# Attention with two expert layers on one core: a list schedule that prices the shared SBUF port and a half clock at the start

## The chip, the cores and the metric

The kernel runs on one core of a Trainium2 chip. The metric is the device time of one execution in microseconds (us), the median of several runs. Engines are named as in the profile: PE is TensorE's matrix multiply and PEld its weight load, DVE is VectorE, ACT is ScalarE, POOL is GpSimd, SP is SyncE, which issues the DMAs.

## The reference

B = 4 batches, 8 heads, 576 positions, 64 columns per head; q and k are drawn eight times larger than v.

```python
# pooled attention: mean over 4 neighbours, softmax attention on 144 positions, repeated 4 times
q_d = q.reshape(B, H, Sd, factor, D).mean(axis=3)      # the same for k_d, v_d
out_up = np.repeat(sm_attn(q_d, k_d, v_d), factor, axis=2)
# local attention: a band of 7 keys around each position
mask = np.abs(pos[:, None] - pos[None, :]) < factor
out_local = softmax(np.where(mask, q @ k.T / 8, -1e9)) @ v
x = (out_up + out_local)                               # as 2304 tokens x 512
...
h = x @ w_in;  g = s * relu(h) ** 2 + b;  y = g @ w_out        # layer 1, 512 -> 2048 -> 512
h = y @ w_in2; g = h - np.tanh(h);        out = g @ w_out2     # layer 2, the same sizes
```

## The kernel before

The 2304 tokens are worked in eight blocks u of 288. Each block's x is written as two parts, xh (high) and xl (low, what xh leaves over), so that products of a faster number format keep their accuracy; X[u] is ready when the last xl is written. Blocks 0 and 1 are one batch, whose attention runs on TensorE with narrow products at the start: transposes tokT of the loaded q and k (L543), scores S (L573, L575) and pooled scores Sd (L614), transposed softmax weights PT and PdT (L588, L634), products with V O and up (L598, L644), and the transposes xt (L655). Among these stand warm-ups (warm, L853), products of the identity with itself whose result isn't used: 14 at first and 16 later, where the kernel's text places them. Each is two rows of the trace.

For blocks 2 to 7 the local attention runs elementwise. VectorE makes most products of Q and K (pD, L181), GpSimd some (pP, L181), VectorE sums both by rows into s (L186), then come a softmax and the products with V (pD and pP at L249, pA on ScalarE at L245), which VectorE adds into O (L257). The pooled attention of these batches takes reductions pp (L353), maxima nm (L398) and sums E on VectorE. At the end xq adds both (L314) and VectorE subtracts xl (L318).

Layer 1 runs on TensorE while later blocks are still in attention: ph is x times the first weights (L735, twelve products per slice i of 128 hidden columns: xh, xl with the two parts of the weight), ScalarE squares the relu into gh, VectorE makes its low part gl (L756), and acc collects gh and gl times the second weights (L768), which yst takes away (L783 to L791). The weights are split into their parts at L697 to L723. Layer 2 (L1000 to L1016 and L735 for yxh, yxl) follows behind 600 us.

Every engine executes its own list in order. These lists are not the order of the text: list_schedule reckons through the whole program with one cost per instruction from cost(), takes for each engine that comes free the ready instruction of the highest priority (the text's place), and pin_order makes the resulting order binding. What it reckons decides only the order; when an instruction really starts, semaphores decide. The words of the start and the warm-ups' places stand in these lines:

```python
RING = '0p1s2ps'
WARM0 = 14
WARM_AT = 'efpu'
...
def warm(n):
    for _ in range(n):
        pe.matmul(warm_t[:, :128], ident, ident, start=True, stop=True)
```

and what a round of list_schedule picks, in these:

```python
_, n = heapq.heappop(ready[e])
i = by[n]
order[e].append(n)
```

Of the kernel before, what the change touches and what calls it, by code (L numbers as in the profile page):

```python
# [1066 lines left out]
ENG = {"PE": 55, "Activation": 34, "DVE": 33, "Pool": 78, "SP": 30}  # L1067
ISSUE = 450.0
BW = 300.0


def cost(i, reads, writes):
    e = i.engine.name
    w = writes[0]
    n = 1
    for ap in [*reads, *writes]:
        k = 1
        for _, c in list(ap.ap)[1:]:
            k *= c
        n = max(n, k)  # L1080
    if i.opcode == "DMACopy":
        return ISSUE, 0.0
    if e == "PE":
        n = 1
        for _, c in list(w.ap)[1:]:
            n *= c
        if "float32r" in str(reads[0].dtype):
            t = (n + 32) / 2.4
        elif i.is_transpose:
            t = 64.0 if n <= 72 else 110.0  # L1090
        else:
            t = 1.2 * n
        return t, t + 162
    if e == "Activation":
        t = 170 + 0.85 * n
        if len([r for r in reads if r is not reads[0]]) and n < 200:
            t += 115
        return t - 110, t
    if e == "DVE":
        t = 140 + 1.05 * n  # L1100
        if i.opcode == "TensorReduce" and list(reads[0].ap)[-1][0] != 1:
            t *= 1.7
        return t - 80, t
    t = 140 + 2.35 * n
    return t - 60, t


def issue_order(tc, nc):
# [129 lines left out]
def list_schedule(ins, dep, soft, aps):  # L1238
    import heapq
    by = {i.name: i for i in ins}  # L1240
    eng = {n: i.engine.name for n, i in by.items()}
    left = {n: len(d) + len(soft[n]) for n, d in dep.items()}
    nxt = {n: [] for n in dep}
    for n, d in dep.items():
        for m in d:
            nxt[m].append((n, False))
        for m in soft[n]:
            nxt[m].append((n, True))
    ready, later = {e: [] for e in ENG}, {e: [] for e in ENG}
    free, at, order = {e: 0.0 for e in ENG}, {n: 0.0 for n in dep}, {e: [] for e in ENG}  # L1250
    key = {i.name: (i.bass_priority, k) for k, i in enumerate(ins)}
    wake = [(0.0, e) for e in ENG]
    dma = 0.0
    for n in by:
        if not left[n]:
            heapq.heappush(later[eng[n]], (0.0, key[n], n))
    heapq.heapify(wake)
    while wake:
        t, e = heapq.heappop(wake)
        if t < free[e]:  # L1260
            continue
        while later[e] and later[e][0][0] <= t:
            _, k, n = heapq.heappop(later[e])
            heapq.heappush(ready[e], (k, n))
        if not ready[e]:
            if later[e]:
                heapq.heappush(wake, (later[e][0][0], e))
            continue
        _, n = heapq.heappop(ready[e])
        i = by[n]  # L1270
        order[e].append(n)
        if i.opcode == "RegisterMove":
            busy, end = 30.0, t
        else:
            busy, end = cost(i, *aps[n])
            end += t
        if i.opcode == "DMACopy":
            size = 4
            for _, c in list(aps[n][1][0].ap):
                size *= c  # L1280
            dma = max(dma, t + 1300.0) + size / BW
            end = dma + 900.0
        free[e] = max(t + busy, dma - 2000) if e == "SP" else t + busy
        heapq.heappush(wake, (free[e], e))
        todo = list(nxt[n])
        while todo:
            m, order_only = todo.pop()
            if m not in by:
                left[m] -= 1
                if not left[m]:  # L1290
                    todo += nxt[m]
                continue
            if order_only:
                go = t
            elif eng[m] == e and i.opcode != "DMACopy":
                go = t if e == "PE" else end + 32
            else:
                go = end + ENG[eng[m]]
            at[m] = max(at[m], go)
            left[m] -= 1  # L1300
            if not left[m]:
                heapq.heappush(later[eng[m]], (at[m], key[m], m))
                heapq.heappush(wake, (max(at[m], free[eng[m]]), eng[m]))
    assert sum(map(len, order.values())) == len(ins)
    return order


def pin_order(tc, nc):
    ins, dep, soft, aps = issue_order(tc, nc)
    order = list_schedule(ins, dep, soft, aps)  # L1310
    by = {i.name: i for i in ins}
    behind = mybir.DependencyInfo(mybir.DependencyClass.NoSync, mybir.DependencyReason.DATA)
    for l_ in order.values():
        for a, b in zip(l_, l_[1:]):
            tc.add_manual_dep(by[b], a, behind, reason="issue order")
# [30 lines left out]
```

## Time and profile before

| what | before |
|---|---|
| median of three runs | 976.96 us |
| the runs | 973.97, 976.96, 979.11 us |
| the profiled execution's own time | 974.62 us |
| its span (first to last instruction) | 972.8 us |
| TensorE busy | 929.2 us, 96% |
| VectorE busy | 616.8 us, 63% |
| ScalarE busy | 453.3 us, 47% |
| GpSimd busy | 166.4 us, 17% |

The span is what the trace shows; 1.8 us of the execution's own time lie around it. The share of an engine is a mean over the whole span and hides stages: VectorE is full in the first 40% and half idle later. An instruction's duration in the trace is from its start to its end, so it holds what it waits inside for something shared.

### The profile page before, as it was taken

Reading aid. Unit: us, or ns where it says so; the run is one execution under the profiler, and the core shown is the slowest. Engines: PE = TensorE matmul, PEld = TensorE weight load, DVE = VectorE, ACT = ScalarE, POOL = GpSimd, SP = SyncE. Lnnn points to the kernel's source line nnn. Section 1 sums busy time; section 2 is a strip of 40 time slices with the busy share of each in tenths; the row PEclk is TensorE's granted clock in tenths of the full one; section 3 lists DMA queues with packets and bytes.
Section 4 is the critical chain, followed back from the end, with each engine's and each line's share of the span. In section 5 each row is a group of like instructions: output and inputs, shape, how many; then the busy total and the mean of one; then the engine's idle time right before and its main releaser. Section 6 shows DMA issues by size and latency. Waiting matters only on the chain.

```text
span 972.8 us, 15109 instructions
## 1 busy us (share of the span) xinstructions
PE 929.2 (96%) x5786; PEld 830.7 (85%) x5786; DVE 616.8 (63%) x966; ACT 453.3 (47%) x1216; POOL 166.4 (17%) x128
## 2 busy tenths in 40 slices
PE   9989999899899899899999999999999999999998
PEld 8778988799788789899899989888888888888886
DVE  5788899999999999996775983322332232222222
ACT  5789746345547374556585962221322232122221
POOL 1553533233225233251000000000000000000000
PEclk9579999999999999999999999999999999999999
DMA  9990323223130322310173850000110000001001
GB/s 232 308 356 2 130 87 126 78 86 126 54 126 26 96 84 78 101 54 1 47 260 136 322 144 11 22 1 1 43 44 1 1 26 19 0 1 44 1 1 43
DMA packets 57966, 80.72 MB, mean 83 GB/s; under 512 B 21046, under 2 KB 42790, under 8 KB 57894
## 3 DMA queue, kind: packets, MB, share of 16 engines
q1 hardware_dynamic: 57510, 79.24, 25.5%
q8 instruction: 45, 0.74, 0.3%
q10 hardware_dynamic: 384, 0.52, 0.2%
q14 instruction: 27, 0.22, 0.1%
HBM read 69.72 MB, written 10.03 MB: 82 GB/s over the span
## 4 chain that ended last, share of the span: by engine, by line
PE 70%; DVE 20%; issue 5%; ACT 3%; POOL 0%; DMA 0%; SPq 0%; DVEq 0%; POOLq 0%; ACTq 0%
PE ph L735 33%; PE acc L1016 20%; PE acc L768 11%; DVE O L257 2%; DVE s L186 2%; DVE pD L181 2%; DVE pp L353 2%; DVE gl L756 2%; DVE xq L314 1%; DVE pD L249 1%; DVE wf L715 1%; DVE xl L318 1%; PE warm L853 1%; DVE O L249 1%; PE O L598 1%
## 5 line engine op out<-in xcount | busy, mean ns | idle before, releaser
L735 PE MATMUL ph<-xh,w 128*128 128x288 f32 x1024 | 239.3, 307 | 7.6 <-DVE gl L756 6.1
L768 PE MATMUL acc<-gh,w 128*128 128x288 f32 (+1 forms) x1024 | 228.1, 298 | 3.7 <-DVE yst L791 2.1
L735 PE MATMUL ph<-yxh,w 128*128 128x512 f32 (+1 forms) x640 | 194.0, 369 | 0.0
L1001 DVE TENSOR_TENSOR ph<-ph,th 128x512 f32<-128x512 f32 (+1 forms) x80 | 51.5, 645 | 224.0 <-ACT th L1000 224.0
L735 PEld LDWEIGHTS ph<-xh,w 128*128 128x128 f32 x1024 | 176.6, 194 | 16.0 <-DVE gl L756 9.2
L1016 PE MATMUL acc<-w,gx 128*128 128x512 f32 x768 | 185.4, 391 | 0.0
L768 PEld LDWEIGHTS acc<-gh,w 128*128 128x128 f32 x1024 | 171.7, 189 | 6.1 <-DVE yst L791 3.0
L1016 PEld LDWEIGHTS acc<-w,gx 128*128 128x128 f32 x768 | 144.2, 188 | 31.2
L735 PE MATMUL ph<-xl,w 128*128 128x288 f32 x512 | 156.2, 305 | 8.6 <-DVE xl L318 6.4
L1000 ACT ACTIVATE th<-ph 128x512 f32<-128x512 f32 (+1 forms) x80 | 44.4, 555 | 232.7 <-PE ph L735 232.6
L768 PE MATMUL acc<-gl,w 128*128 128x288 f32 x512 | 151.2, 296 | 0.0
L735 PEld LDWEIGHTS ph<-yxh,w 128*128 128x128 f32 x640 | 116.9, 188 | 21.8
L735 PE MATMUL ph<-yxl,w 128*128 128x512 f32 (+1 forms) x320 | 118.3, 370 | 0.0
L735 PEld LDWEIGHTS ph<-xl,w 128*128 128x128 f32 x512 | 99.1, 193 | 10.9 <-DVE xl L318 7.1
L768 PEld LDWEIGHTS acc<-gl,w 128*128 128x128 f32 x512 | 97.0, 190 | 0.0
L747 ACT ACTIVATE ph<-ph 128x288 f32<-128x288 f32 x128 | 51.0, 398 | 88.3 <-PE ph L735 88.2
L756 DVE TENSOR_TENSOR gl<-ph,gh 128x288 fp32r<-128x288 f32 x128 | 57.2, 449 | 31.9 <-ACT gh L753 31.3
L735 PEld LDWEIGHTS ph<-yxl,w 128*128 128x128 f32 x320 | 60.2, 188 | 10.7
L1003 DVE TENSOR_TENSOR gx<-ph,gx 128x512 fp32r<-128x512 f32 x64 | 44.2, 690 | 37.8 <-ACT gx L1002 37.8
L245 ACT ACTIVATE pA<-V,a 128x64 f32<-128x64 f32 x198 | 53.7, 343 | 11.3 <-DVE O L257 10.5
L1002 ACT CAST gx<-ph 128x512 fp32r<-128x512 f32 x64 | 37.5, 586 | 44.9 <-DVE ph L1001 44.9
L753 ACT CAST gh<-ph 128x288 fp32r<-128x288 f32 x128 | 50.9, 398 | 7.0 <-PE acc L768 4.1
(137 smaller groups left out, 1200.1 us busy)
## 6 DMA issues: line engine op xcount, KB each, us to landing
wraw<-in_moe_w_in_dram SPq DMA_DIRECT2D x32, 512.0 KB
wraw<-in_moe_w_out_dram SPq DMA_DIRECT2D x32, 512.0 KB
y<-yst SPq DMA_DIRECT2D x36, 144.0 KB
K<-in_k_dram SPq DMA_DIRECT2D x5, 960.0 KB
V<-in_v_dram SPq DMA_DIRECT2D x5, 960.0 KB
Q<-in_q_dram SPq DMA_DIRECT2D x6, 576.0 KB
raw<-in_q_dram SPq DMA_DIRECT2D x24, 144.0 KB
raw<-in_k_dram SPq DMA_DIRECT2D x24, 144.0 KB
```

Source lines behind the costliest of these rows:

```text
L181: eng.tensor_tensor(out=p, in0=Qt[u], in1=Kt[u][:, :, o:o + TAU, :], op=ALU.mult)
L245: act.activation(out=p_[:, t, h], in_=Vt[u][:, h, o + t], func=AF.Copy, scale=st["a"][:, h * TAU + t, o:o + 1])
L735: pe.matmul(p_, w_, x_, start=n == 0, stop=n == 3 * KC - 1)
L747: act.activation(out=p_, in_=p_, func=AF.Relu)
L753: act.copy(out=gh[:, :NB1], in_=p_)
L756: dve.tensor_tensor(out=gl, in0=p_, in1=gh[:, :NB1].bitcast(F32), op=ALU.subtract)
L768: pe.matmul(accs[u][e][:, :g_.shape[1]], w_, g_, start=i == first and n == 0, stop=i == last and n == 2)
L1000: act.activation(out=t, in_=p_, func=AF.Tanh)
L1001: dve.tensor_tensor(out=p_, in0=p_, in1=t, op=ALU.subtract)
L1002: act.copy(out=gh, in_=p_)
L1003: dve.tensor_tensor(out=gl, in0=p_, in1=gh.bitcast(F32), op=ALU.subtract)
L1016: pe.matmul(accs[j][t], g_, w_, start=i == 0 and n == 0, stop=i == NF - 1 and n == 2)
```

## The change

Only the planner changes; the program's instructions are the same. Three things: cost() gets other numbers for ScalarE, VectorE, GpSimd and Memset. The new takes_port() marks the instructions of VectorE and GpSimd that the planner shall let run in turn only: all of GpSimd's but Memset, and VectorE's that touch no PSUM and are no TensorReduce or Reciprocal. While one of them is reckoned to hold the port (held), the other engine takes the best ready instruction that needs no port, or waits; VectorE also gives way where GpSimd has a ready one of higher priority. And up to COLD = 55 us every cost of TensorE counts twice.

```diff
+COLD = 55000.0
...
+    if i.opcode == "Memset":
+        return 50 + 0.8 * n, 100 + 0.8 * n
+    last = [d for d in list(reads[0].ap)[1:] if d[1] > 1]
+    strided = bool(last) and abs(last[-1][0]) > 2
     if e == "Activation":
-        t = 170 + 0.85 * n
-        if len([r for r in reads if r is not reads[0]]) and n < 200:
+        t = 160 + 0.85 * n
+        if len(reads) == 2:
             t += 115
+        elif len(reads) > 2:
+            t += 190
         return t - 110, t
     if e == "DVE":
-        t = 140 + 1.05 * n
-        if i.opcode == "TensorReduce" and list(reads[0].ap)[-1][0] != 1:
-            t *= 1.7
+        t = 130 + 1.05 * n
+        if strided:
+            t *= 1.75 if i.opcode == "TensorReduce" else 1.35
+        elif i.opcode == "TensorScalarPtr" and len(reads) == 1 and not takes_psum(reads):
+            t = 140 + 0.55 * n
         return t - 80, t
-    t = 140 + 2.35 * n
+    t = 200 + 2.07 * n
     return t - 60, t
+
+
+def takes_psum(aps):
+    return any("PSUM" in str(a.bass_ap.tensor._space).upper() for a in aps)
+
+
+def takes_port(i, reads, writes):
+    e = i.engine.name
+    if e == "Pool":
+        return i.opcode != "Memset"
+    if e != "DVE" or i.opcode in ("TensorReduce", "Reciprocal"):
+        return False
+    return not takes_psum([*reads, *writes])
...
-    dma = 0.0
+    dma = held = 0.0
+    port = {n: takes_port(by[n], *aps[n]) if n in by else False for n in dep}
...
-        _, n = heapq.heappop(ready[e])
+        pick = 0
+        if port[ready[e][0][1]]:
+            other = "Pool" if e == "DVE" else "DVE"
+            rival = [k for k, n in ready[other][:1] if port[n] and free[other] <= t]
+            if held > t or e == "DVE" and rival and rival[0] < ready[e][0][0]:
+                open_ = [r for r in ready[e] if not port[r[1]]]
+                if open_:
+                    pick = ready[e].index(min(open_))
+                elif held > t:
+                    heapq.heappush(wake, (held, e))
+                    continue
+        _, n = ready[e].pop(pick)
+        heapq.heapify(ready[e])
...
             busy, end = cost(i, *aps[n])
+            if e == "PE" and t < COLD:
+                busy, end = 2 * busy, 2 * end - 162
+            if port[n]:
+                held = t + end - 40
             end += t
```

What moves is shown at three places. First TensorE's list at its start, before (equal neighbours in one row; warm is the warm-up, tokT a transpose of q or k):

```order
L853 MATMUL warm<-ident 128x128 x14
L543 MATMUL tokT<-ident,tok 128x128 x4
L853 MATMUL warm<-ident 128x128 x2
L543 MATMUL tokT<-ident,tok 128x128 x4
L853 MATMUL warm<-ident 128x128 x3
L543 MATMUL tokT<-ident,tok 128x128 x4
L853 MATMUL warm<-ident 128x128 x3
L543 MATMUL tokT<-ident,tok 128x128 x4
L853 MATMUL warm<-ident 128x128 x4
L543 MATMUL tokT<-ident,tok 128x128 x3
L853 MATMUL warm<-ident 128x128 x4
L543 MATMUL tokT<-ident,tok 128x128 x12
```

and of the change, the list's first rows and then those where the later warm-ups begin (S, Sd are scores, PT transposed weights, O the product with V):

```order
L853 MATMUL warm<-ident 128x128 x14
L543 MATMUL tokT<-ident,tok 128x128 x36
L573 MATMUL S<-bandr,identr 96x408
L575 MATMUL S<-KT,QT 96x102 x4
...
L853 MATMUL warm<-ident 128x128
L614 MATMUL Sd<-kd,qd 72x144 x2
L588 MATMUL PT<-ident,bs 102x96 x8
L853 MATMUL warm<-ident 128x128
L614 MATMUL Sd<-kd,qd 72x144 x2
L588 MATMUL PT<-ident,bs 102x96 x4
L853 MATMUL warm<-ident 128x128 x2
```

The sixteen later warm-ups have moved from between the transposes to between the scores and what follows them.

Second VectorE's list where the x of block 2 is finished (xl_2531 is its low part, s_2658 and pD_2732 belong to the local attention of the next block). Before:

```order
L318 TENSOR_TENSOR xl_2531<-xq_2537,xh_2530 128x4x128
L791 TENSOR_SCALAR yst_2517<-acc_1682,scal_86,bcol_87 128x288
L318 TENSOR_TENSOR xl_2531<-xq_2583,xh_2530 128x4x128
L314 TENSOR_TENSOR xq_2591<-xt_2589,upT_1749 128x4x16 x2
L181 TENSOR_TENSOR pD_2732<-Q_2131,K_2133 128x1152
L756 TENSOR_TENSOR gl_2612<-ph_2596,gh_2611 128x288
L318 TENSOR_TENSOR xl_2531<-xq_2591,xh_2530 128x4x32
L186 TENSOR_REDUCE s_2658<-pD_2732 128x18
```

and with the change:

```order
L318 TENSOR_TENSOR xl_2531<-xq_2537,xh_2530 128x4x128
L186 TENSOR_REDUCE s_2658<-pP_2660 128x18
L318 TENSOR_TENSOR xl_2531<-xq_2583,xh_2530 128x4x128
L314 TENSOR_TENSOR xq_2591<-xt_2589,upT_1749 128x4x16 x2
L786 TENSOR_TENSOR yst_2722<-acc_2564,yst_2722 128x288
L786 TENSOR_TENSOR yst_2727<-acc_2565,yst_2727 128x288
L398 TENSOR_REDUCE nm_2830<-S_2824 72x2
L353 TENSOR_REDUCE pp2_2913<-raw72_2780 72x256
L318 TENSOR_TENSOR xl_2531<-xq_2591,xh_2530 128x4x32
```

Adds yst, a maximum, a pooling reduction and a row reduction of GpSimd's product now stand ahead of the last xl, and the product pD_2732 behind it.

Third VectorE's list behind the row reduction of pP_4996, which frees GpSimd to start its next product of Q and K. Before:

```order
L186 TENSOR_REDUCE s_4994<-pP_4996 128x18
L756 TENSOR_TENSOR gl_4647<-ph_4631,gh_4646 128x288
L181 TENSOR_TENSOR pD_5147<-Q_4546,K_4548 128x1152
L398 TENSOR_REDUCE nm_4669<-S_4663 72x2
L398 TENSOR_REDUCE nm_4669<-S_4666 72x2
```

and with the change:

```order
L186 TENSOR_REDUCE s_4994<-pP_4996 128x18
L181 TENSOR_TENSOR pD_5050<-Q_4546,K_4548 128x1152
L756 TENSOR_TENSOR gl_4828<-ph_4812,gh_4827 128x288
L314 TENSOR_TENSOR xq_4853<-xt_4848,upT_2734 128x4x48
L314 TENSOR_TENSOR xq_4853<-xt_4848,upT_2734 128x4x16 x2
L314 TENSOR_TENSOR xq_4853<-xt_4848,upT_2734 128x4x48
L186 TENSOR_REDUCE s_4994<-pD_5050 128x18
```

A product pD stands directly behind the reduction now, with a gl and the adds xq, which read PSUM, behind it.

## Rows read from the trace of the kernel before

**Rows 1.** The page: busy time by engine, and TensorE's granted clock in 40 slices

```profile
PE 929.2 (96%) x5786; PEld 830.7 (85%) x5786; DVE 616.8 (63%) x966; ACT 453.3 (47%) x1216; POOL 166.4 (17%) x128
...
PEclk9579999999999999999999999999999999999999
```

**Rows 2.** Busy us of PE, PEld, DVE, ACT, POOL by stretch; granted clock, DMA

```profile
60.00:118.00 58.00, 56.77 (x467) 52.57 (x466) 49.08 (x104) 50.70 (x137) 25.44 (x20) 1.00 0.34 125
118.00:206.00 88.00, 80.48 (x582) 73.59 (x581) 82.09 (x112) 40.87 (x136) 29.77 (x29) 0.96 0.32 102
206.00:419.00 213.00, 193.27 (x1451) 183.51 (x1451) 207.55 (x271) 116.76 (x392) 68.14 (x29) 0.98 0.26 84
419.00:600.00 181.00, 176.97 (x1313) 171.76 (x1312) 132.53 (x242) 118.17 (x306) 15.75 (x6) 1.00 0.37 129
```

**Rows 3.** The same view for short stretches of the start

```profile
8.00:12.00 4.00, 4.00 (x39) 4.00 (x38) 1.70 (x3) 2.21 (x2) 0.00 (x0) 1.00 1.36 219
24.00:28.00 4.00, 3.98 (x21) 2.73 (x21) 2.12 (x8) 4.00 (x18) 1.55 (x2) 0.73 1.00 250
28.00:36.00 8.00, 8.00 (x56) 7.13 (x56) 4.01 (x16) 5.12 (x16) 4.86 (x5) 0.50 0.90 290
56.00:60.00 4.00, 4.00 (x18) 4.00 (x18) 2.77 (x7) 2.88 (x9) 2.36 (x2) 0.50 1.02 409
```

**Rows 4.** Timeline of PE, start: start and duration in us, what, idle before

```profile
1.45 5.26 PE L853 MATMUL warm<-ident 128*128 128x128 f32 x28 [1.45 <-POOL ident L108]
6.55 0.60 PE L543 MATMUL tokT<-ident,tok 128*128 128x128 f32 x4
6.99 0.61 PE L853 MATMUL warm<-ident 128*128 128x128 f32 x4
...
19.55 0.87 PE L588 MATMUL PT<-ident,bs 96*102 96x96 f32 x8
...
24.55 1.64 PE L588 MATMUL PT<-ident,bs 96*102 96x96 f32 x8
...
54.37 0.61 PE L735 MATMUL ph<-xl,w 128*128 128x288 f32 x1 [2.20 <-DVE xl L663]
```

**Rows 5.** Timeline of DVE, 373 to 381 us

```profile
375.32 3.68 DVE L181 TENSOR_TENSOR pD<-Q,K 128x1152 f32<-128x1152 f32 x1
```

**Rows 6.** Timeline of POOL, 360 to 385 us

```profile
375.12 2.67 POOL L181 TENSOR_TENSOR pP<-Q,K 128x1152 f32<-128x1152 f32 x1 [4.18 <-DVE s L186]
```

**Rows 7.** Groups of DVE by form: count, busy us, mean ns; idle before

```profile
L181 DVE TENSOR_TENSOR pD<-Q,K 128x1152 f32<-128x1152 f32 x30 | 50.2, 1672 | 0.0
L353 DVE TENSOR_REDUCE pp<-raw 72x256 f32<-72x1024 f32 x24 | 48.1, 2010 | 0.0
L186 DVE TENSOR_REDUCE s<-pD 128x18 f32<-128x1152 f32 x30 | 40.4, 1346 | 0.2
...
L398 DVE TENSOR_REDUCE nm<-S 72x2 f32<-72x288 f32 x24 | 9.9, 445 | 1.7 <-PE S L391 1.7
...
L786 DVE TENSOR_TENSOR yst<-acc,yst 128x288 f32<-128x288 f32 x4 | 1.7, 471 | 0.0
```

**Rows 8.** Lines L181 and L257 by operation: ns min/median/max, first and last start

```profile
L181 DVE TENSOR_TENSOR pD<-Q,K x30: 1318/1349/3679, 118.7 to 439.7; 128x1152 f32<-128x1152 f32 x30
...
L257 DVE TENSOR_TENSOR O<-O,pA x11: 1342/1884/3036, 192.0 to 478.4; 128x1152 f32<-128x1152 f32 x11
```

**Rows 9.** Waits of PE in 206 to 419 us: total us, times, longest us

```profile
PE ph L735 <- DVE xl L318: 6.4, 3, 3.1
PE ph L735 <- DVE gl L756: 5.1, 6, 1.4
PE xt L296 <- DVE O L257: 2.3, 1, 2.3
```

**Rows 10.** Timeline of DVE: block 2's last xl, and a late gl

```profile
206.00 0.33 DVE L318 TENSOR_TENSOR xl<-xq,xh 128x128 fp32r<-128x128 f32 x1
...
418.20 0.46 DVE L756 TENSOR_TENSOR gl<-ph,gh 128x288 fp32r<-128x288 f32 x1
```

## The prediction

> **What bounds the kernel now.** The page's busy shares come first [rows 1]: TensorE is busy 929 of 972.8 us, VectorE 617. TensorE's clock row shows where that is misleading: in the second and third slice (24 to 73 us) the granted clock is 0.5 and 0.7. The table of stretches [rows 2] then separates the stages. From 60 to 118 us TensorE is busy 56.8 of 58 us. From 118 to 206 and from 206 to 419 us VectorE is busy 82.1 of 88 and 207.6 of 213 us, and TensorE loses 7.5 and 19.7 us. After 419 us TensorE loses 4.0 us up to 600 and next to nothing later. So the tail is TensorE's own work, which this change doesn't touch; it can win or lose time at the start (TensorE at the half clock) and in 118 to 419 us (VectorE sets the pace). The list of waits of TensorE in 206 to 419 us names VectorE: xl, the low half of the next block's x, 6.4 us, and gl, 5.1 us [rows 9].
>
> Why is VectorE so full? [Rows 5, 6] show one case. GpSimd's product pP runs 2.67 us from 375.12; VectorE's product pD of the same size starts 0.2 us behind it and takes 3.68 us, against a median of 1.35 [rows 8]. The mean of its group is 1672 ns over 30 [rows 7]; the adds O<-O,pA have a median of 1884 over 11 against a quickest of 1342 [rows 8]: 30 x 0.32 + 11 x 0.54 = 15.5 us lost in two groups. The same difference over all VectorE groups, each against its quick tenth, comes to 53 us, nearly all of it on operations that the new test takes_port marks and under 1 us on the others. The new test thus describes a real cost; the question is what the new order does with it.
>
> **The change, part by part.** No instruction is added or removed; only the order on each engine moves. The cost lines (a few per cent on each duration) have no price of their own.
>
> *Start.* In the old order 16 of the 30 warm-up products stand between the first transposes; in the new one, with TensorE's costs doubled up to 55 us, the 36 transposes stand in one piece and those 16 come later, between the scores. Three prices follow. (a) The transposes take 0.11 us each (4 in 0.44 us, from the starts in [rows 4]) and wait for their loads; without the warm-ups TensorE is mostly idle from 8 to 12 us, where the old order had it busy 4.00 of 4 us [rows 3]. In the old run the clock fell to half inside 24 to 28 us, where TensorE was busy 3.98 of 4 us [rows 3] (a mean of 0.73 over these 4 us puts the fall at 25.9), once the warm-ups were over and only narrow products were left. So I expect it to fall at about 12. What TensorE does from 12 to 25.9 us then goes at half clock: a group of eight PT rows takes 1.64 instead of 0.87 us [rows 4], so 13.9 us times 1.64/0.87 - 1 is +12; part of these narrow products is paced by other engines, and I take +11. (b) 16 warm-ups are 32 of the rows that took 5.26/28 = 0.19 us each at half clock [rows 4]: +6. (c) The old order gives back up to 3.5 us (32 x 0.11 at full clock, in part time in which the loads were awaited anyway; I take 2), and of the idle time of TensorE between 26 and 54 us, about 5 us (2.20 of it in front of the first xl product, [rows 4]), all is filled: -7. The first layer's products, which start in earnest at 54.4 us [rows 4], start at about 64: +10. Bounds: 0 (the clock holds) and +17 (nothing is given back). From 60 to 118 us TensorE loses only 1.2 us [rows 2], so little can be caught up there; the new order places 3 us less of weight splitting before the fifth gl, and I give back 2: +8 at 118 us.
>
> *118 to 206 us, up to the x of block 2.* The last xl of block 2 (at 206.00 us, [rows 10]) now has 7.0 us more VectorE work ahead of it: four adds yst (0.47 each), a pooling reduction (2.01), two row reductions (1.35 each) and a maximum (0.45) [rows 7]. Another 1.1 us moved from before 118 us to behind it. Stalls: I take each GpSimd product, the VectorE instruction that releases it, and the VectorE work behind that which needs no port; what is missing to GpSimd's 2.67 us [rows 6] is the stall of the next VectorE operation that does. Over 23 products of the old order this reckoning gives 30.9 us; the trace shows 29.2 on the same products, so it holds. In this stretch it gives 5.9 measured before and 2.2 after, -3.7. Together 7.0 + 1.1 - 3.7 = +4.4: block 2's x comes at +12, some 218 us instead of 206.
>
> *206 to 419 us, blocks 2 to 5.* VectorE has 18 us less to do up to a late gl of block 5 (the one at 418.20 us, [rows 10]): the 7.0 us just paid, and 11.2 us of block 7's attention (seven operations of 1.35 us, [rows 7], and the small ones of a softmax) that now stand behind it, where VectorE is busy only 132.5 of 181 us [rows 2] and so hides them. Loads keep their lead: each Q, K and V load of these blocks still has 19 us or more of VectorE work between its release and its first use. Stalls by the same reckoning: 20.5 measured before, 10.9 after; one product is read 2 us after its release and costs 1.5 back: -8. VectorE's part is thus -26 us. TensorE can't take all of it: it loses 19.7 us here [rows 2], of which the list names 14 for xl, gl and O [rows 9]; I take that, -14. Behind 419 us the order is nearly the same: 0.
>
> Sum: +8 +4.4 -14 = -1.6 on the profiled execution's 974.6 us, 973.0. That execution lies 2.3 us under the median of 976.96, so the median to expect is 975. The kernel's own runs span 974 to 979 us; under 0.5% (4.9 us) can't be told from no change.
>
> **A rule that speaks against my first term.** Rows: between 28 and 36 us TensorE was busy all of 8 us, and the clock stayed at 0.50; it was still 0.50 from 56 to 60 us and 1.00 from 60 us on, with the layer's full-width products under way since 54.4 us [rows 2 to 4]. The Trainium skill, TensorE: Matmul & The Clock Gate, Part 1, has the throttled state as the default, which sustained activity of the engine lifts. By that page the warm-ups strewn between the scores would keep TensorE active and bring the full clock back by themselves, and the sum would be 8 us lower; the rows at 28 to 36 us speak against it. It is the first rival.
>
> **Rivals.** 1, faster: the full clock holds through the start, or returns before the first layer. For it: full-width warm-ups now stand among the narrow products. Against it: the half clock of 28 to 36 us. Start 0 instead of +8, that is 967. 2, faster: TensorE takes the whole 19.7 us in 206 to 419 and not 14, 969; with both, 961. For it: all its long waits there are for VectorE. Against: the other third are short gaps with other releasers. 3, slower, by one mechanism: the port. The order is fixed, the moments are not; if GpSimd's products start elsewhere than the planner thought, the stalls stay at some 53 us. Then block 2's x is late by 8 + 7.0 + 1.1 = 16 us; in 206 to 419 VectorE is relieved of the 18 us of moved work alone, without the 8 of stalls, and TensorE's gain there is the same share of that, 14 x 18/26 = 10: 974.6 + 16 - 10 = 981, median 983. It decides if the stalls stay above some 45 us. 4, same: the change does nothing because the reckoned stalls only change places: it lies inside the forecast's range.
>
> **How the numbers follow.** Forecast, same: 0.38. Rivals 1 and 2 together, faster: 0.35. Rival 3, slower: 0.27. The likeliest is 975, its own range 971 to 981. The range that holds 8 in 10 reaches from both gains at once (961) to rival 3 with half of what the start's upper bound adds to it (983 + 9/2): 960 to 988.
>
> **What the profile after would show.** Start: the clock row falls near 12 us, and the first L735 stands near 64 us; if it stands near 54, the first term was wrong. The mean of pD should fall from 1672 to some 1500 ns, and the whole excess of VectorE from 53 to about 40 us. The last xl of block 2 near 218 us; that late gl of block 5 (418.20 before) within 3 us of its place. The waits of TensorE for xl and gl from 11.5 us to under 5. Behind 600 us every row shifts alike. I am wrong if the clock doesn't fall early, if the excess on VectorE doesn't shrink, or if TensorE's idle time in 206 to 419 stays near 20 us.

## The result and the profile after

The change makes the kernel faster by 1.1%: 966.39 us median (964.77 to 968.11 in four runs) against 977.82 us; the ratio is 0.989, interval 0.9855 to 0.9925. The profiled execution took 967.31 us with a span of 965.5 us, 7.3 us less than the span before; the one before lay at the low end of its kernel's runs, so the medians are further apart than the traces. The time lies inside the predicted range, but not where the likeliest case put it (975, no change, with 971 to 981 as its own range). Rivals 1 and 2 named faster; of these rival 2 came nearest, and even its 19.7 us are less than what was won there.

The page of the changed kernel, busy time and clock, answers to [rows 1]:

```profile
PE 938.6 (97%) x5786; PEld 840.9 (87%) x5786; DVE 596.7 (62%) x966; ACT 456.2 (47%) x1216; POOL 154.7 (16%) x128
...
PEclk7559999988999999999999999999999999999999
```

The same 966 instructions keep VectorE busy 20.1 us less. The clock is half for longer at the start, and lower again in the ninth and tenth slice.

Busy time by stretch (PE, PEld, DVE, ACT, POOL, then clock), answers to [rows 2]; the last two divide the third:

```profile
60.00:118.00 58.00, 57.16 (x436) 51.27 (x436) 44.50 (x104) 46.61 (x126) 22.43 (x17) 0.91 0.27 100
118.00:206.00 88.00, 87.11 (x659) 81.64 (x657) 79.99 (x115) 46.33 (x147) 34.21 (x34) 1.00 0.35 112
206.00:419.00 213.00, 202.87 (x1538) 194.79 (x1537) 201.39 (x291) 123.43 (x409) 59.08 (x30) 0.97 0.28 89
419.00:600.00 181.00, 175.60 (x1278) 169.25 (x1277) 139.66 (x241) 116.05 (x298) 16.43 (x7) 0.99 0.37 129
...
206.00:225.00 19.00, 10.99 (x46) 9.01 (x46) 18.60 (x28) 7.02 (x20) 7.81 (x4) 0.64 0.41 129
225.00:419.00 194.00, 191.87 (x1494) 185.78 (x1492) 182.78 (x264) 116.40 (x389) 51.27 (x26) 1.00 0.27 85
```

TensorE loses 0.9 us in 118 to 206 us, where it lost 7.5. Then comes one hole, 206 to 225 us, with 8.0 us idle and a clock of 0.64; behind it, up to 419 us, only 2.1 us are lost. VectorE is no longer full there: 182.8 of 194 us.

The start, first by short stretches and then on TensorE's timeline, answers to [rows 3, 4]:

```profile
8.00:12.00 4.00, 1.72 (x13) 1.07 (x11) 2.79 (x4) 2.00 (x2) 0.00 (x0) 1.00 1.31 223
12.00:16.00 4.00, 2.91 (x15) 2.63 (x15) 0.92 (x2) 1.73 (x2) 0.00 (x0) 0.59 1.06 309
28.00:36.00 8.00, 8.00 (x37) 6.45 (x37) 4.18 (x8) 6.40 (x20) 7.42 (x7) 0.50 0.97 298
60.00:70.00 10.00, 10.00 (x42) 7.86 (x42) 8.27 (x19) 6.45 (x17) 1.94 (x4) 0.50 1.02 390
```

```profile
31.66 0.79 PE L853 MATMUL warm<-ident 128*128 128x128 f32 x2
...
67.64 0.61 PE L735 MATMUL ph<-xl,w 128*128 128x288 f32 x1
```

TensorE is busy 1.72 of 4 us from 8 to 12 us, and the mean of 0.59 in the next 4 us puts the fall of the clock at 12.7 us. It stays at 0.50 through the later warm-ups and past 70 us. The first xl product of layer 1 comes at 67.64 us instead of 54.37.

VectorE's products of Q and K and the adds of pA, by line (ns min/median/max), answer to [rows 8]; the reductions s, which the rule marks as free of the port, stand beside them:

```profile
L181 DVE TENSOR_TENSOR pD<-Q,K x30: 1324/1348/4008, 132.0 to 458.0; 128x1152 f32<-128x1152 f32 x30
...
L257 DVE TENSOR_TENSOR O<-O,pA x11: 1345/1348/3314, 203.0 to 483.1; 128x1152 f32<-128x1152 f32 x11
...
L186 DVE TENSOR_REDUCE s<-pD x30: 1332/1344/1385, 139.9 to 459.3; 128x18 f32<-128x1152 f32 x30
```

The median of the adds is back at the quickest (1884 before); single products still stall, up to 4.0 us. The reductions never do: 1385 ns is the longest of 30, and the nine of them that run beside a GpSimd operation of over 1 us take at most 1348. Of the 30 products pD, 17 ran beside such an operation before, and 7 do now. Those that run beside none take at most 1403 ns before and 1390 now, so every longer one met GpSimd. By the Trainium skill, SBUF — State Buffer, "Who interferes with whom", VectorE with two SBUF inputs contends with a GpSimd instruction that reads SBUF, and a tensor reduction doesn't. The trace agrees on both.

TensorE's waits in 206 to 419 us answer to [rows 9]:

```profile
PE xt L296 <- DVE O L257: 4.9, 1, 4.9
PE ph L735 <- DVE gl L756: 1.2, 3, 0.5
...
PE ph L735 <- DVE xl L318: 0.2, 1, 0.2
```

The waits for xl and gl fell from 11.5 to 1.4 us. What is left is one wait for the attention of block 2, with which the hole behind 206 us begins:

```profile
210.97 1.94 PE L296 MATMUL xt<-ident,O 128*128 128x128 f32 x8 [4.94 <-DVE O L257]
```

### The profile page after: what moved, and what is told of

The parts are those of the page before. It is cut to its first block, busy times and chain, and to the rows that moved or that the text cites. A ratio compares the mean times of both kernels' runs of the same rounds, so it can differ in the third digit from the quotient of the medians.

```text
span 965.5 us, 15135 instructions
## 1 busy us (share of the span) xinstructions
PE 938.6 (97%) x5786; PEld 840.9 (87%) x5786; DVE 596.7 (62%) x966; ACT 456.2 (47%) x1216; POOL 154.7 (16%) x128
## 4 chain that ended last, share of the span: by engine, by line
PE 75%; DVE 12%; ACT 7%; issue 3%; DMA 2%; SPq 1%; DVEq 0%; ACTq 0%
PE ph L735 34%; PE acc L1016 20%; PE acc L768 12%; ACT pA L245 2%; PE S L575 2%; DVE s L186 2%; DVE xq L314 1%; DVE pD L181 1%; PE O L598 1%; DVE gl L756 1%; DVE wf L715 1%; DMA wraw<-in_moe_w_in_dram 1%; DVE O L257 1%; SPq L502 1%; ACT E L401 1%
## 5 line engine op out<-in xcount | busy, mean ns | idle before, releaser
L735 PE MATMUL ph<-xh,w 128*128 128x288 f32 x1024 | 235.2, 304 | 2.8 <-DVE gl L756 2.1
L735 PE MATMUL ph<-yxh,w 128*128 128x512 f32 (+1 forms) x640 | 194.2, 369 | 0.6 <-DVE gl L1003 0.6
L735 PEld LDWEIGHTS ph<-xh,w 128*128 128x128 f32 x1024 | 174.0, 191 | 9.0 <-DVE gl L756 4.0
L735 PE MATMUL ph<-xl,w 128*128 128x288 f32 x512 | 154.4, 302 | 0.2 <-DVE xl L318 0.2
```

The lines of the kernel that those rows point to most:

```text
L735: pe.matmul(p_, w_, x_, start=n == 0, stop=n == 3 * KC - 1)
```

## The experiments

Three parts of the change can be switched apart: the new cost numbers, the port rule (`port` all false without it) and the doubled costs (`COLD = 0` without them). Theory 1, the prediction's: the port rule earns time from block 2 on, the doubled costs lose some at the start, and the two add up. Theory 2: a late start is given back before block 2's x. Theory 3: the doubled costs themselves earn the gain. Each kernel was timed in five rounds beside the kernel before.

**e1, new costs and port rule.**

```diff
-COLD = 55000.0
+COLD = 0.0
```

> The new costs and the port rule, without the doubled costs of TensorE at the start (COLD = 0). Theory 1 (the port rule earns the gain, the doubled costs lose some 10 us at the start, and both add up): first xl product of layer 1 near 55 us, VectorE busy some 597 us as in the changed kernel, time some 10 us under the changed kernel, about 957. Theory 2 (a late start is given back, since TensorE would wait for VectorE between 118 and 419 us anyway): the same start, but TensorE idle some 10 us more in that stretch, time about 966. Theory 3 (the doubled costs themselves earn the gain): about 977.

Measured: 969.05 us, ratio 0.9904 (0.9886 to 0.9921); VectorE busy 598.3 us; first xl product at 59.7 us. The start was 8 us better than in the changed kernel, the time no better: 12 us above theory 1 and 3 above theory 2.

**e2, the doubled costs alone.**

```diff
-    port = {n: takes_port(by[n], *aps[n]) if n in by else False for n in dep}
+    port = {n: False for n in dep}
```

and cost() as before.

> Only the doubled costs of TensorE up to 55 us; old costs, no port rule. Theory 1: clock falls near 12 us, first xl product near 67 us, VectorE busy about 617 us as before, some 10 us slower than before, about 987. Theory 2: the same start, the same VectorE, but TensorE waits some 7 us less in 118 to 419 us: 978 to 981. Theory 3: about 966.

Measured: 977.28 us, ratio 0.9993 (0.998 to 1.0007); VectorE busy 611.3 us; first xl product at 68.7 us. Theory 3 falls. The late start cost nothing here, as theory 2 has it, though VectorE was busy 5.5 us less than before, which theory 2 didn't expect.

**e3, the port rule alone** (`COLD = 0`, cost() as before).

> Only the port rule; old costs, no doubling. Theory 1: VectorE busy 600 us or less, TensorE idle between 118 and 419 us halved from 27 to 11 us or less, about 960. Theory 2: VectorE busy falls by the same, about 966. Theory 3: about 977 with VectorE busy near 617.

Measured: 979.71 us, ratio 1.0012 (0.9999 to 1.0025), though VectorE was busy only 599.0 us. So all three theories miss: the stalls were removed and no time was won.

**e4, the new costs alone** (`COLD = 0`, `port` all false).

> Only the new numbers in the cost function; no port rule, no doubling. Theories 1 to 3: within 4 us of the kernel before (about 977), VectorE busy within 5 us of 617. If it moves by more than 8 us either way, any new order of these lists moves the time as much as the whole change does, and the parts can't be added.

Measured: 977.33 us, ratio 0.9986 (0.9971 to 1.0002); VectorE busy 615.3 us. As expected.

**e5, warm-ups early.** The planner runs as in the changed kernel; then, in TensorE's list alone, the later warm-ups (w_l) go behind the transposes (t_l) at which they stood before.

```diff
     order = list_schedule(ins, dep, soft, aps)
...
+    pe_l = [n for n in pe_l if n not in set(w_l[WARM0:])]
...
+    for k, c in ((4, 2), (8, 3), (12, 3), (16, 4), (19, 4)):
+        p = pe_l.index(t_l[k - 1]) + 1
+        pe_l[p:p] = w_l[:c]
+        w_l = w_l[c:]
+    order["PE"] = pe_l
```

> The changed kernel, with its sixteen later warm-ups back at the places among the transposes that they had before; every other list is word for word that of the changed kernel. If the predicted first term is right in its cause (warm-ups late, clock falls early), the clock falls near 24 us instead of 12.7 and the first xl product of layer 1 comes some 10 us earlier than 67.6. Theory 1 (the start's loss adds to the end): 956 to 958. Theory 2 (it is given back before the x of block 2): 964 to 968, with TensorE idle some 10 us more between 60 and 225 us.

Measured: 959.11 us, ratio 0.9806 (0.979 to 0.9822). Its stretches and the first xl product:

```profile
8.00:12.00 4.00, 4.00 (x39) 4.00 (x38) 1.70 (x3) 2.21 (x2) 0.00 (x0) 1.00 1.29 221
...
18.00:24.00 6.00, 6.00 (x31) 4.53 (x30) 4.15 (x8) 4.39 (x15) 0.59 (x1) 0.59 1.12 219
```

```profile
60.01 0.61 PE L735 MATMUL ph<-xl,w 128*128 128x288 f32 x1
```

The clock falls at 19.1 us instead of 12.7 (0.59 over 18 to 24 us; 24 was expected), the first xl product comes 7.6 us earlier, and the end 7.3 us earlier by the medians (8.6 by the profiled executions). That is 1.1 us above theory 1's range and 5 us under theory 2's. Nothing else in the lists moved, and from the first gl on both stages of the table below take the same time to within 0.2 us. So in the changed kernel's order this part of the start's loss adds in full. What e2 got back (10.6 us between its first and 33rd gl) it got in another order of all lists; TensorE is idle 4.9 us less there than before, so slack may have had a share in e2.

**e6, the doubling up to 62 us.**

```diff
-COLD = 55000.0
+COLD = 62000.0
```

> The changed kernel with the doubled costs up to 62 instead of 55 us: the start keeps its order, but the last xl of block 2 has 6.0 us less VectorE work ahead of it. If that work is what made TensorE idle around 211 us: the last xl of block 2 near 214 instead of 220.4, TensorE idle there 9 us less by half, time 960 to 963. If something else sets block 2's x: 965 to 969. Either way it shows how far a small change of the plan scatters the time.

Measured: 962.37 us, ratio 0.9835 (0.982 to 0.9851). The hole behind 206 us has gone:

```profile
206.00:225.00 19.00, 17.40 (x125) 15.52 (x124) 18.62 (x30) 10.68 (x30) 7.95 (x3) 1.00 0.38 121
```

TensorE is busy 17.4 of 19 us there instead of 11.0, at full clock; block 2's last xl ends at 216.7 us instead of 220.4. A part was lost earlier, 4.6 us between the first and the 17th gl, and one stall has gone too: the add O<-O,pA that took 3.31 us at 203 us in the changed kernel takes 1.35 here. So the 3.7 us aren't the moved work's alone.

**e7, new costs and doubling, no port rule; e8, port rule and doubling, old costs.**

> New costs and doubled start costs, but no port rule. If the port rule is needed for the gain: VectorE busy 610 us or more, time about 976. If new costs and a late start were enough: 967 with VectorE busy near 617.

> Port rule and doubled start costs, with the old costs. If the rule needs the new costs (durations that fit what the port is held): VectorE busy near 600 but time about 977. If the port rule with a late start is enough: 966 to 969.

Measured: e7 984.75 us, ratio 1.0066 (1.0051 to 1.008), VectorE busy 609.8 us; e8 966.33 us, ratio 0.988 (0.9865 to 0.9895), VectorE busy 593.1 us. The rule is needed; with the doubling on, the new costs are not. Without the rule e7 is 9 us slower even than expected.

**e9, e5 and e6 together.**

> The two changes of e5 and e6 together: doubled costs up to 62 us, and the sixteen later warm-ups at their old places. If the start's gain and the earlier x of block 2 are separate, both add: 959.1 - 4.0, about 955, first xl product near 60 us. If the earlier start only makes TensorE wait for VectorE: 959 to 962.

Measured: 954.2 us, ratio 0.9768 (0.9746 to 0.9789), the fastest of all. The two add: 959.1 - 4.0 = 955.1 was expected. Its page and its stretches:

```profile
PE 928.9 (98%) x5786; PEld 831.0 (87%) x5786; DVE 594.6 (62%) x966; ACT 456.2 (48%) x1216; POOL 152.8 (16%) x128
```

```profile
206.00:419.00 213.00, 209.21 (x1603) 199.64 (x1604) 200.60 (x289) 128.09 (x424) 64.30 (x30) 1.00 0.26 84
```

TensorE loses 3.8 us in the stretch where it lost 19.7 before.

**e10, the moved work alone.** The plan of before, with one dependence more for the 14 VectorE operations (late_u6: a softmax, products and adds of block 6, 11.2 us) that the changed kernel puts behind the late gl.

```diff
+    for k in late_u6:
+        soft[f"I-{k}"].add(gl)
     order = list_schedule(ins, dep, soft, aps)
```

> The kernel before, in whose plan only the 14 VectorE operations of block 6 that the changed kernel puts behind the late gl of block 5 (11.2 us) are held back behind that gl; no new costs, no port rule, no doubling. If the moved work earned the gain from block 2's x on: that gl some 10 us earlier (408 instead of 418) and 967 to 970. If the port's stalls earned it: 975 to 979, with VectorE busy near 617 as before.

Measured: 979.6 us, ratio 1.0018 (1.0003 to 1.0033); VectorE busy 618.1 us. The time was won and lost again. First TensorE's stretches, before and in e10, then its waits in front of block 6's x in e10:

```profile
340.00:419.00 79.00, 72.03 (x544) 68.60 (x543) 77.73 (x99) 46.45 (x159) 26.84 (x12) 0.98 0.27 88
419.00:500.00 81.00, 78.66 (x598) 75.88 (x597) 61.52 (x105) 49.32 (x154) 15.75 (x6) 1.00 0.21 69
```

```profile
340.00:419.00 79.00, 75.39 (x583) 72.37 (x582) 69.60 (x105) 44.37 (x149) 21.21 (x11) 1.00 0.29 94
419.00:500.00 81.00, 73.80 (x543) 70.71 (x542) 68.62 (x96) 48.15 (x158) 18.79 (x8) 0.96 0.16 50
```

```profile
465.61 0.61 PE L735 MATMUL ph<-xh,w 128*128 128x288 f32 x1 [2.99 <-ACT xh L317]
467.23 0.61 PE L735 MATMUL ph<-xl,w 128*128 128x288 f32 x1 [1.01 <-DVE xl L318]
```

TensorE loses 3.6 us in 340 to 419 us (7.0 before), and 7.2 us in 419 to 500 us (2.3 before), where block 6's x now comes late (467.2 us, 462.3 before).

**e11, the rule with VectorE's marks turned round; e12, e9 without the rule.**

```diff
-    if e != "DVE" or i.opcode in ("TensorReduce", "Reciprocal"):
-        return False
-    return not takes_psum([*reads, *writes])
+    if e != "DVE":
+        return False
+    return i.opcode in ("TensorReduce", "Reciprocal") or takes_psum([*reads, *writes])
```

> The kernel of e9 with the rule's marks on VectorE turned round: its reductions, reciprocals and operations on PSUM count as taking the port, the others not. The plan is disturbed as much as by the true rule, and less urgent VectorE work is moved back as well (8 us less ahead of block 5's last xl than before), but what stalls on the chip isn't kept apart. If the gain is the port's: VectorE busy 608 us or more, VectorE's products slow as before, time 968 to 980. If any such reordering would do: 954 to 960.

> The kernel of e9 without the port rule (new costs, doubling up to 62 us, warm-ups at their old places). If the port rule earns most of e9's gain: VectorE busy 608 us or more, TensorE idle 15 us or more between 206 and 419 us, time 972 to 980. If warm-ups, costs and doubling do: 954 to 962.

Measured: e11 1012.53 us, ratio 1.0355 (1.033 to 1.038), VectorE busy 623.8 us; e12 992.39 us, ratio 1.0156 (1.0134 to 1.0179), VectorE busy 619.9 us. Both are slower than any theory said. The stretch of 206 to 419 us, e11 and then e12:

```profile
206.00:419.00 213.00, 188.82 (x1385) 179.76 (x1384) 195.02 (x259) 112.06 (x365) 66.31 (x28) 0.93 0.26 84
```

```profile
206.00:419.00 213.00, 193.93 (x1423) 185.03 (x1424) 206.12 (x285) 114.01 (x380) 63.81 (x29) 0.94 0.27 89
```

TensorE loses 24.2 and 19.1 us there, at a lower clock. Without the rule or with the wrong one the stalls are back. Both lose at the start too: the first gl comes 25.0 and 9.0 us later than in e9. TensorE waits there for VectorE's and ScalarE's work on the first batch (5.5 us at once for bE in e11); why e12, with its warm-ups early, has its first gl hardly earlier than e7 (75.1 and 75.7 us) and takes 9.1 us longer from there to the 33rd was not settled.

The table holds what the traces of all fourteen kernels show: VectorE's busy time from the page, the end of the 1st of layer 1's 128 gl, and the times from there to the end of the 33rd and from the 33rd to the 81st (16 gl to a block, so these two are the first of blocks 2 and 5). The rule is "port".

| kernel | parts | VectorE busy | 1st gl | 1st to 33rd | 33rd to 81st | median |
|---|---|---|---|---|---|---|
| before | none | 616.8 | 60.0 | 150.5 | 197.7 | 977.8 to 978.4 |
| e4 | costs | 615.3 | 62.4 | 155.2 | 193.2 | 977.3 |
| e2 | doubling | 611.3 | 75.9 | 139.8 | 194.3 | 977.3 |
| e7 | costs, doubling | 609.8 | 75.7 | 145.3 | 194.9 | 984.8 |
| e10 | moved work | 618.1 | 61.7 | 150.6 | 192.1 | 979.6 |
| e12 | e9 without port | 619.9 | 75.1 | 154.4 | 194.2 | 992.4 |
| e11 | e9, port turned round | 623.8 | 91.1 | 147.5 | 199.2 | 1012.5 |
| e3 | port | 599.0 | 61.5 | 166.6 | 182.3 | 979.7 |
| e1 | costs, port | 598.3 | 65.4 | 159.4 | 178.8 | 969.1 |
| e8 | port, doubling | 593.1 | 71.8 | 155.7 | 178.7 | 966.3 |
| after | all three | 596.7 | 73.4 | 151.9 | 172.4 | 966.4 |
| e5 | all, warm-ups early | 601.4 | 65.8 | 151.9 | 172.3 | 959.1 |
| e6 | all, to 62 us | 592.2 | 73.0 | 147.9 | 176.4 | 962.4 |
| e9 | e5 and e6 | 594.6 | 66.1 | 148.0 | 175.9 | 954.2 |

The rule parts the kernels in two columns: VectorE busy 592 to 601 us with it and 610 to 624 without, and 172 to 182 us against 192 to 199 from the 33rd to the 81st gl. No other part does that. Nor does a late start of this stage: e9 and e2 reach the 33rd gl at 214.1 and 215.7 us and then take 175.9 and 194.3. From the 1st to the 33rd gl the rule costs time: 16.1 us alone, 15.9 with the doubling, 4.2 with the new costs, 6.6 with both. That is why the rule alone won nothing. Part of that price in e3 is one wait of 2.96 us for a softmax of the start on VectorE (bE), with the clock at half right behind it, from 80 to 90 us:

```profile
79.68 0.42 PE L634 MATMUL PdT<-ident,bE 72*72 72x72 f32 x4 [2.96 <-DVE bE L630]
```

```profile
80.00:90.00 10.00, 8.56 (x39) 7.84 (x38) 4.94 (x9) 7.57 (x23) 2.81 (x2) 0.51 0.01 2
```

Weight splitting stands ahead of this softmax: its maximum on VectorE starts 1.0 us behind its scores, and the next step on ScalarE 1.7 us behind the maximum. The rest of the price was not followed to its causes.

## Why the prediction was right and where it failed

- **Start, +10 at the first xl product and +8 at 118 us.** Right in mechanism, near in size, and that in part by luck: +13.3 at the first xl product, and by the gl around 118 us +7 to +11 (the 13th came 10.9 us later, the 17th 7.9). The clock fell at 12.7 us (forecast 12). e5 shows the cause: with the warm-ups back, 7.6 us of the 13.3 go, and by the medians 7.3 count at the end. The other 5.7 us belong to the rest of the new order at the start, which the forecast didn't price; even with the warm-ups back the clock falls 6.8 us earlier than before, and why stays open. The 0.19 us of price (b) is a mean over two rates, 0.21 us a row at first and 0.11 later; the 32 late rows held TensorE for 8.9 us, not 6.
- **Rival 1, the clock holds or comes back early.** Wrong: the later warm-ups stand between 31.7 and 58 us and the clock is 0.50 there, with TensorE busy 8 of 8 us from 28 to 36 us. The Trainium skill, TensorE: Matmul & The Clock Gate, Part 1, would have sustained activity lift the throttle; these rows don't show it, by busy time as the profile counts it.
- **118 to 206 us, +4.4 and block 2's x at +12.** Right, and somewhat small: the last xl of block 2 ended at 220.4 us, +14.1 (forecast 218, before 206.3). From the first to the 33rd gl the stage grew by 1.5 us (151.9 against 150.5): 5.5 us were given back up to the 17th, and 7.0 lost behind it. The reason holds as well: VectorE's timeline has the work that the forecast counted, ahead of the last xl.

```profile
206.22 1.34 DVE L186 TENSOR_REDUCE s<-pD 128x18 f32<-128x1152 f32 x1
...
217.19 0.82 DVE L786 TENSOR_TENSOR yst<-acc,yst 128x288 f32<-128x288 f32 x2
...
218.28 1.95 DVE L353 TENSOR_REDUCE pp<-raw 72x256 f32<-72x1024 f32 x1
220.15 0.28 DVE L318 TENSOR_TENSOR xl<-xq,xh 128x128 fp32r<-128x128 f32 x1
```

  e6, with 6.0 us of it taken away, has the last xl 3.7 us earlier and is 4.0 us faster, though in e6 this work isn't all that differs.
- **206 to 419 us: the step that failed.** The forecast gave VectorE -26 us and TensorE only -14, because "TensorE can't take all of it". It took all: from the 33rd to the 81st gl the stage is 25.3 us shorter. The cap was read from the idle time that the list of waits names. Worked out over that stage, TensorE's idle time fell by 17.4 us, from 19.5 to 2.1; the half-clock time that had followed its waits fell from 6.8 us to none, which is 3.4 us of work; and the 4.5 us that remain were busy time, of fewer products (1321 rows in the stage, 1337 before) and of products that take less. So beside the half clock the forecast's 14 had left out 3.4 us of idle time and these 4.5. With the sum's other terms the late gl was to come 13.6 us earlier by VectorE's reckoning and 1.6 by TensorE's; it came 11.6 earlier (406.56 instead of 418.20 us), so the forecast "within 3 us of its place" was wrong too.

```profile
406.56 0.44 DVE L756 TENSOR_TENSOR gl<-ph,gh 128x288 fp32r<-128x288 f32 x1
```

- **What makes up the -26.** The forecast had 18 us of moved work and 8 of stalls. The 11.2 us (which belong to block 6; the prediction calls it block 7) don't pay by themselves: e10 holds back just these, wins 5.6 us from the 33rd to the 81st gl and loses 7.4 on the next 16, since block 6's x is due. So VectorE doesn't hide them behind the late gl as long as all the stalls are there, and what the stalls would give was under-sized: VectorE's whole busy time fell by 20.1 us, and by the prediction's way of counting the excess in 206 to 419 us fell by 13. In the changed kernel, with fewer stalls, the same move costs no wait: block 6's x comes 50.1 us behind the late gl instead of 44.1, but still earlier than before (456.7 us, before 462.3), and TensorE waits for no xl there.
- **Behind 419 us, 0.** From the late gl to the end the changed kernel takes 4.3 us longer (558.9 against 554.6), and one wait accounts for it: 2.5 us up to 436.3 us, for a softmax of the pooled attention on VectorE, with the clock at half for 3.4 us behind it, which is 1.7 us of work. Missed, and small.
- **Rival 3, the stalls stay.** Wrong for the reason it gave as its condition: they fell from 53 to some 32 us. Counted anew from the traces, each of VectorE's groups against its 10th percentile, the excess is 55 us before and 33 after on the operations that the rule marks, and 4.7 and 4.1 on the others, where the prediction has under 1. The mean of pD fell from 1672 to 1508 ns, as forecast.

Sum of the traces: +13.4 at the first gl, +1.5, -25.3, and +3.3 from the 81st gl to the last: -7.1, against 7.3 less span. The forecast's sum was -1.6. It is luck that it misses by 5.7 us and not by the 11.3 of the capped term: what lies ahead of block 2's x and behind the late gl was some 3 us too small each, which made up for half.

## What to carry over

A planner that knows which instructions exclude each other on two engines pays, but price the whole list: alone the rule won nothing, because it lost in front of block 2 what it won behind it. Don't cap a gain at the idle time that a list of waits names: here half-clock stretches stood behind the longer waits, short gaps went as well, and some busy time with them. And when one part of a planner's change is suspected, move only those instructions in the finished lists, as e5 did; a changed plan moves everything else too.

## What was not expected of the hardware

Turning the marks round cost 58 us against e9 (1012.5 and 954.2), twice the 29 us of VectorE's busy time between them. The place of sixteen warm-up products, whose result nobody reads, was worth 7.3 us. The half clock behind a wait of TensorE had very different lengths in three cases: 13.7 us behind the 4.9 us at 206 us in the changed kernel, 10.2 us behind the 2.96 us at 77 us in e3, both with narrow or interrupted products following, but 3.4 us behind the 3.1 us at 398 us in the kernel before, with the layer's products following. That what follows sets the length was not tested.
